# Expert tiles of a fused attention and mixture kernel: how many buffers each pool has, in which slots the loads are emitted, and both halves of the second expert layer ahead of the first combine

## The chip, the cores and the metric

One core of one Trainium2 chip runs the whole program. The metric is the device time of one execution in microseconds. Before the change the median of three runs is 944.0 us (943.19 to 945.39).

## What is computed

Three layers follow one another. The sizes are 4 batches, 8 heads, 768 positions, 64 per head, so 3072 tokens of 512 features.

```python
# 1. attention with 4 sink positions and a window of 128
keep = is_sink | ((rel >= 0) & (rel < window))
a = softmax(where(keep, q @ k.T / sqrt(64), -1e9)); x = a @ v        # (3072, 512)
# 2. gated layer, d_ff 1536
x = (sigmoid(x @ w_gate) * (x @ w_val)) @ w_out
# 3. soft mixture: 8 experts of 4 slots
logits = x @ phi                                                     # (3072, 32)
slot_in = softmax(logits, axis=0).T @ x                              # (32, 512)
for e in range(8): slot_out[e] = relu(slot_in[e] @ w1[e]) @ w2[e]    # w1 512x1024, w2 1024x512
out = softmax(logits, axis=1) @ slot_out                             # (3072, 512)
```

## The kernel before, in words

**Halves and passes.** The tokens are worked in 8 halves of 384 (half of a batch). The gated layer goes in five passes over the 12 chunks of its hidden features (128 each): half 0, halves 1 and 2, 3 and 4, 5 and 6, half 7 (line 437). Each pass loads its 36 weight tiles of 256 KB anew. They are numbered by chunk over all passes: g50, v50 and o50 are the tiles of the gate, the value and the output weight of chunk 50, and the last pass has chunks 48 to 59. Every tile comes by a DMA on SP's queue into one of three buffers `raw` (line 462), ACT copies its high part and POOL makes the low part by subtraction (lines 494 and 495); the buffer is then free for the load three tiles on. The products with the gate and value tiles are L632, those with the output tiles L670.

**Slots.** A list `ops` written out by hand (lines 593 to 596) holds 354 operations, each of them one group of L632 or L670. The main loop (line 1033) goes through it, and in every slot it also emits, where they are due, attention pieces, pieces of the third layer's logits and sums for a finished half (`m2`, lines 688 to 756), a splitting of `x`, one start of a weight tile with the next load, and at most one load of an expert tile (lines 1070 to 1073). The last pass begins in slot 294; a step of one chunk there is five slots.

**Order on the queues.** What the loop writes is the program's order only. The context is opened with `schedule_with_timeline_sim=True` (line 1137), and the order in which the instructions stand on each engine is fixed when the program is built; only those marked `pin` keep the order in which they are written. On the chip every engine then works off its queue in that order.

**Expert tiles.** The weights of the experts are 32 tiles of 1 MB (8 KB in each partition), in the order of line 801: 16 of `w1` (rows of 2 KB), then 8 of the left half of `w2` and 8 of its right half (rows of 1 KB). `NX = [10, 5, 8]` gives the number of buffers of three pools. Pool `xe0` opens when the attention is done and its memory is given back (line 1063; slot 290), and lies where the attention's tiles were. Pool `xe1` opens when the pass before the last is done (line 1067; slot 306). It begins where `xe0` ends, and its five tiles reach over the memory of `gv2`, `gv3` and `o3`, weight pools of the earlier passes. Behind those lie `ye` (the layer's output of the even halves) and `x0` (the input of every other half). Pool `x2` opens in the tail, on the memory of the last pass, from `x0` upwards. The 15 tiles of the first two pools are loaded in the loop, the other 17 in the tail: 8 into `x2`, then 9 into buffers 1 to 9 of `xe0` again as the first expert layer is done with them (lines 1083 to 1087). Buffer 0 takes the activations (`big`).

**Tail.** The last half's `m2` (its last step adds to `acc`, L752), then the weights of the combination (L828 to L833), the first expert layer (L857), and for each of two column halves c: `second(c)` (L878, then a small product L885 and copies L883 to L889 that make `S4[c]`), `combine(c)` (L896: 12 pairs of products, one copy each by DVE or ACT in turns, L900, and a store of 768 KB after every third, L902). The eight output tiles `ob` use the buffers of `x2`, each its own.

```python
        for q in range(len(xe)):
            if 32 - len(e_order) in range(sum(NX[0:q]), sum(NX[0:q + 1])):
                e_load(e_tile(xe[q], f"e{q}", NX[q]))
                break
```

Of the kernel before, what the change touches and what calls it, by code (L numbers as in the profile page):

```python
# [36 lines left out]
def fused_kernel(ctx, tc, qT, kA, kB, vB, vS, wg, wv, wo, phi, w1, w2, n_sink, window, out):  # L37
# [10 lines left out]
    def ps(tag, bufs, dt=F32):  # L48
        return psum.tile([128, 512], dt, name=tag, tag=tag, bufs=bufs)
# [122 lines left out]
    def tick():  # L172
        run = []
        for e in pend:
            e[0] -= 1
            if e[0] <= 0:
                run.append(e)
        for e in run:
            pend.remove(e)
            e[1]()  # L180
# [7 lines left out]
    def copy(eng, o, i):  # L188
        if eng is act:
            act.copy(o, i)  # L190
        else:
            eng.tensor_copy(o, i)  # L192
# [364 lines left out]
    def x_can():  # L557
        k = xs_n[0]
        return k < NH and k - 2 < xused[0] and done_half[0] > x_order[k]
# [238 lines left out]
    e_order = deque()  # L798
# [16 lines left out]
    def e_tile(pl, tag, bufs):  # L815
        return pl.tile([128, 2048], F32, name="ew", tag=tag, bufs=bufs)
# [6 lines left out]
    def combine_weights(cp, cT):  # L823

        for h in range(NH):
            c4 = cp.tile([128, 3, 4, 32], F32R, name="c4", tag="c4", bufs=2)
            cb = c_all[:, h].unsqueeze(2).to_broadcast([128, 3, 2, 32])
            dve.tensor_copy(c4[:, :, 0::2, :], cb)  # L828
            dve.tensor_tensor(c4[:, :, 1::2, :], cb, c4[:, :, 0::2, :].bitcast(F32), op=ALU.subtract)
            t = ps(("xt", "pt")[h % 2], 1)  # L830
            for i in range(3):
                pe.transpose(t[:, 128 * i:128 * i + 128].bitcast(F32R), c4[:, i].rearrange("p a b -> p (a b)"), identr)
            act.copy(cT[:, h, :], t[:, 0:384])  # L833

    def tail(ta, cp, big, outs):

        cT = cp.tile([128, NH, 384], F32R, name="cT")
        combine_weights(cp, cT)
        A = ta.tile([128, 2, 4, 4, 32], F32, name="A")
        pool.memset(A, 0.0)  # L840
        si_ps = ps("gv", 3)
        for d in range(4):
            pe.matmul(si_ps[:, 32 * d:32 * d + 32], acc[:, 128 * d:128 * d + 128], Rf[:, 0, :], start=True, stop=True,
                      skip_group_check=True)
        for g in range(2):
            dve.tensor_tensor(
                A[:, g, :, :, 4 * g:4 * g + 4],
                si_ps[:, 0:128].rearrange("p (d g j s) -> p g j d s", d=4, g=2, j=4)[:, g],
                zi.rearrange("p (g j s) -> p g j s", g=2, j=4)[:, g].unsqueeze(2).to_broadcast([128, 4, 4, 4]), op=ALU.mult)

        hTs = big().rearrange("p (g f r) -> p g f r", g=2, f=8)
        for g in range(2):
            hp = [ps("ys", 3) for _ in range(2)]
            for nn in range(2):
                for d in range(4):
                    for j in range(4):
                        pe.matmul(hp[nn][32 * j:32 * j + 32, :], A[:, g, j, d, :], xp[0, g, 4 * nn + d][:, j, :],  # L857
                                  start=(d == 0), stop=(d == 3), skip_group_check=True)
            hT = hTs[:, g]
            for nn in range(2):  # L860
                hs = ta.tile([128, 512], F32, name="hs", tag="hs", bufs=2)
                if nn:
                    act.activation(out=hs, in_=hp[nn], func=ACTF.Relu)
                else:
                    dve.tensor_scalar(hs, hp[nn], 0.0, None, op0=ALU.max)
                t = ps("gv", 3)
                for f in range(4):
                    pe.transpose(t[:, 128 * f:128 * f + 128], hs[:, 128 * f:128 * f + 128], ident)
                copy((dve, act)[nn], hT[:, 4 * nn:4 * nn + 4, :], t.rearrange("p (a b) -> p a b", a=4))

        S4 = {}

        def second(c):
            so = ps(("xt", "pt")[c], 1)
            for f in range(8):
                for g in range(2):
                    for j in range(4):
                        pe.matmul(so[32 * j:32 * j + 32, 0:256], hTs[:, g, f, 32 * j:32 * j + 32], xp[1, c, f][:, 4 * g + j, :],  # L878
                                  start=(f == 0 and g == 0), stop=(f == 7 and g == 1), skip_group_check=True)

            hs = ta.tile([128, 512], F32, name="hs", tag="hs", bufs=2)
            sos, S4h = hs[:, 0:256], hs[64:128, 256:512].bitcast(F32R)
            dve.tensor_copy(sos, so[:, 0:256])  # L883
            s4 = ps("ys", 3)
            pe.matmul(s4[:, 0:256], R2.rearrange("p a b -> p (a b)"), sos, start=True, stop=True)  # L885
            S4[c] = ta.tile([128, 256], F32R, name="S4", tag="S4", bufs=2)
            act.copy(S4h, s4[64:128, 0:256])
            dve.tensor_copy(S4[c][0:64], s4[0:64, 0:256])
            dve.tensor_tensor(S4[c][64:128], s4[64:128, 0:256], S4h.bitcast(F32), op=ALU.subtract)  # L889

        def combine(c):
            for t in range(NBLK // 2):
                o = ps("gv" if t % 2 else "ys", 3)
                for r in range(2):
                    h, i = divmod(2 * t + r, 3)
                    pe.matmul(o[:, 256 * r:256 * r + 256], cT[:, h, 128 * i:128 * i + 128], S4[c], start=True, stop=True,  # L896
                              skip_group_check=True)
                if t % 3 == 0:
                    ob = outs(NBLK // 6 * c + t // 3)[:, 0:1536].rearrange("p (r c) -> p r c", r=6)
                copy(act if t % 2 else dve, ob[:, 2 * (t % 3):2 * (t % 3) + 2, :], o.rearrange("p (r c) -> p r c", r=2))  # L900
                if t % 3 == 2:
                    sp.dma_start(out=out[256 * t - 512:256 * t + 256, 256 * c:256 * c + 256].rearrange("(r p) c -> p r c", p=128), in_=ob)  # L902

        for c in range(2):
            second(c)
            combine(c)


# [118 lines left out]

    setup_merge()
    credit = 0.0
    NX = [10, 5, 8]  # L1030
    xe = []
    e_reset()
    for k, (si, o, i) in enumerate(ops):
        phase[0] = steps[si][0][0] // NF
        if o == "y":
            if si:
                gemm2(si - 1, i)
        else:
            gemm1(si, i, o)
        tick()  # L1040
        now[0] = k + 1
        rate = 0.0
        for h in range(NH):
            todo = half_at[h] - emitted[0] - credit
            if todo > 0 and due[h] > now[0]:
                rate = max(rate, todo / max(due[h] - (3 if h == 1 else 5) - now[0], 1))
        credit += rate
        while credit >= 1:
            credit -= 1
            attn_piece()  # L1050
        if m2:
            m2_piece()
            if si == NS - 1:
                m2_piece()
        if x_can():
            x_split()
        if at_tasks:
            run_split()
        w_slot()
        if not xe and len(tops) == 1 and ws_n[0] >= 3 * NF and not w_fly:  # L1060
            top.close()
            tops.append(top.enter_context(tc.tile_pool(name="parts", bufs=1)))
        if not xe and not pieces and xs_n[0] == NH:
            top.close()
            left.close()
            xe.append(ctx2.enter_context(tc.tile_pool(name="xe0", bufs=1, reuse_waits="tile")))
        if len(xe) == 1 and min(gdone[0], ydone[0]) >= N_LEAN - 1 and m2_done[0] == NH - 1:
            inner.close()
            xe.append(ctx2.enter_context(tc.tile_pool(name="xe1", bufs=1, reuse_waits="tile")))
        for q in range(len(xe)):  # L1070
            if 32 - len(e_order) in range(sum(NX[0:q]), sum(NX[0:q + 1])):
                e_load(e_tile(xe[q], f"e{q}", NX[q]))
                break
    for i in range(3):
# [6 lines left out]
    ta = ctx2.enter_context(tc.tile_pool(name="ta", bufs=1, side="right", reuse_waits="tile"))  # L1081
    x2 = ctx2.enter_context(tc.tile_pool(name="x2", bufs=1, side="right", reuse_waits="tile"))
    for i in range(NX[2]):
        e_load(e_tile(x2, f"e2{i}", 1))
    big = e_tile(xe[0], "e0", NX[0])
    e_all(xe[0], "e0", NX[0], NX[0] - 1)
    e_all(xe[1], "e1", NX[1], 32)
    tail(ta, x2, lambda: big, lambda n: e_tile(x2, f"e2{n}", 1))
    ctx2.close()
    with tc.If(fast == 0):  # L1090
        general()
# [50 lines left out]
```

## Time and profile before

| | |
|---|---|
| median of 3 runs | 944.0 us |
| the profiled execution | 944.22 us |
| its span in the profile | 942.3 us |
| PE busy (products) | 898.0 us, 95% |
| DVE, POOL, ACT busy | 598.7, 475.9, 372.4 us |
| DMA | 133.40 MB, 142 GB/s in the mean |
| chain that ended last | PE 78%, DVE 8%, DMA 4%, issue 4%, ACT 3% |

PE is TensorE's products and PEld its weight loads; SPq is SP's queue, on which all DMAs of this kernel stand. The chain that ended last is followed back from the last instruction, at each step to what released it. The span lies 1.9 us below the time of the same execution. "Granted clock" (PEclk) is the share of full speed that TensorE had.

### The profile page before, as it was taken

How to read it: one execution, taken by the hardware profiler on the slowest of the kernel's cores; microseconds unless marked ns; L12 is line 12 of the kernel's file. 1: busy time of each engine (PE TensorE's matmuls, PEld its weight loads, DVE VectorE, ACT ScalarE, POOL GpSimd, SP SyncE). 2: the span in 40 equal slices, each digit the busy share in tenths (PEclk: the TensorE clock that was granted, in tenths of full speed). 3: DMA queues.
4: the chain of work that ended last, by engine and by line, in shares of the span. 5: the costliest groups of instructions: out<-in, count | busy, mean ns of one | idle time of the engine just before them, and what ended most of it. 6: DMA issues, size and time to landing. Idle time of an engine off the chain costs nothing.

```text
span 942.3 us, 15253 instructions
## 1 busy us (share of the span) xinstructions
PE 898.0 (95%) x5276; PEld 712.5 (76%) x5277; DVE 598.7 (64%) x1536; ACT 372.4 (40%) x996; POOL 475.9 (51%) x428
## 2 busy tenths in 40 slices
PE   8789998989999999999999999999999999899894
PEld 4455554556789999888889999898999987798452
DVE  8996869666558757765776767766455533444532
ACT  5675565333343343344343443343332323241221
POOL 3753445463346675655675756654644422684000
PEclk7799999999999999999999999999999999999897
DMA  6884657531213232333232333231212169656997
GB/s 230 285 268 154 226 173 230 165 100 44 68 54 103 82 106 54 106 84 99 59 105 68 98 78 96 77 101 55 79 57 68 45 211 387 230 155 196 310 323 236
DMA packets 80355, 133.40 MB, mean 142 GB/s; under 512 B 6800, under 2 KB 38544, under 8 KB 80272
## 3 DMA queue, kind: packets, MB, share of 16 engines
q1 hardware_dynamic: 80272, 132.37, 46.1%
q8 instruction: 43, 0.70, 0.3%
q14 instruction: 40, 0.33, 0.1%
HBM read 116.62 MB, written 15.73 MB: 140 GB/s over the span
## 4 chain that ended last, share of the span: by engine, by line
PE 78%; DVE 8%; DMA 4%; issue 4%; ACT 3%; POOL 1%; SPq 0%; POOLq 0%; DVEq 0%; ACTq 0%
PE gv L632 39%; PE ys L670 20%; PE ys L300 4%; PE xt L392 4%; DMA wraw<-wsv 2%; PE ys L857 2%; PE pt L367 2%; DVE wA L517 2%; DVE wA L518 1%; PE ys L697 1%; PE xt L395 1%; PE ys L706 1%; DVE wA L521 1%; PE xt L878 1%; DMA wbits<-in_wv_dram 1%
## 5 line engine op out<-in xcount | busy, mean ns | idle before, releaser
L632 PE MATMUL gv<-xh,whv 128*128 128x384 f32 x432 | 151.6, 379 | 3.2 <-ACT whv L190 3.2
L632 PE MATMUL gv<-xh,whg 128*128 128x384 f32 x432 | 153.1, 383 | 0.0
L670 PE MATMUL ys<-who,gh 128*128 128x512 f32 x324 | 140.2, 460 | 7.8 <-DVE ysb L675 6.3
L649 POOL TENSOR_TENSOR gl<-th,gh 128x384 fp32r<-128x384 f32 x84 | 89.3, 1063 | 111.8 <-DVE gh L192 95.0
L675 DVE SCALAR_TENSOR_TENSOR ysb<-ys,ysb 128x512 f32<-128x512 f32 x138 | 93.0, 683 | 37.8 <-PE ys L670 37.1
L632 PE MATMUL gv<-xh,wlv 128*128 128x384 f32 x336 | 114.3, 340 | 0.7 <-POOL wlv L495 0.7
L632 PE MATMUL gv<-xl,whv 128*128 128x384 f32 x336 | 114.3, 340 | 0.0
L632 PE MATMUL gv<-xl,whg 128*128 128x384 f32 x336 | 114.0, 339 | 0.0
L632 PE MATMUL gv<-xh,wlg 128*128 128x384 f32 x336 | 113.3, 337 | 0.0
L321 ACT ACTIVATE PC<-P,nb 128x132 f32<-128x132 f32 (+1 forms) x152 | 60.2, 397 | 109.0 <-DVE P L315 77.7
L670 PE MATMUL ys<-wlo,gh 128*128 128x512 f32 x252 | 99.5, 395 | 0.0
L670 PE MATMUL ys<-who,gl 128*128 128x512 f32 x252 | 98.4, 396 | 0.0
L632 PEld LDWEIGHTS gv<-xh,whv 128*128 128x128 f32 x432 | 81.3, 190 | 20.0 <-issue 6.4
L327 POOL TENSOR_TENSOR PC<-PC,sm 128x264 f32<-128x264 f32 (+1 forms) x76 | 50.3, 663 | 90.4 <-DVE sm L326 68.3
L632 PEld LDWEIGHTS gv<-xh,whg 128*128 128x128 f32 x432 | 81.7, 191 | 16.0 <-issue 4.7
L495 POOL TENSOR_TENSOR wlv<-wraw,whv 128x512 fp32r<-128x512 f32 x48 | 63.0, 1313 | 58.6 <-ACT whv L190 54.0
L670 PEld LDWEIGHTS ys<-who,gh 128*128 128x128 f32 x324 | 60.2, 189 | 36.6 <-issue 18.2
L645 DVE SCALAR_TENSOR_TENSOR th<-th,gv 128x384 f32<-128x384 f32 x84 | 46.3, 551 | 61.4 <-PE gv L632 50.5
L495 POOL TENSOR_TENSOR wlg<-wraw,whg 128x512 fp32r<-128x512 f32 x48 | 62.5, 1302 | 34.1 <-ACT whg L190 26.9
L304 DVE CUSTOM_DVE_ANT_0 P<-ys,mask 128x260 f32<-128x260 f32 (+1 forms) x152 | 57.2, 392 | 34.1 <-PE ys L300 34.0
L636 ACT ACTIVATE th<-gv 128x384 f32<-128x384 f32 x96 | 46.8, 487 | 80.4 <-PE gv L632 79.8
L325 DVE TENSOR_SCALAR sm<-sm 128x2 f32<-128x2 f32 x96 | 35.9, 374 | 63.5 <-ACT PC L321 57.9
(211 smaller groups left out, 1834.7 us busy)
## 6 DMA issues: line engine op xcount, KB each, us to landing
ew<-in_w_dram SPq DMA_DIRECT2D x32, 1024.0 KB, 12.1
wraw<-wsg SPq DMA_DIRECT2D x48, 256.0 KB, 2.7
wraw<-wsv SPq DMA_DIRECT2D x48, 256.0 KB, 2.7
wraw<-wso SPq DMA_DIRECT2D x48, 256.0 KB, 2.7
wbits<-in_wg_dram SPq DMA_DIRECT2D x12, 512.0 KB, 4.2
wbits<-in_wv_dram SPq DMA_DIRECT2D x12, 512.0 KB, 4.6
wbits<-in_wo_dram SPq DMA_DIRECT2D x12, 512.0 KB, 4.7
out_dram<-ew SPq DMA_DIRECT2D x8, 768.0 KB, 6.8
```

Of the source, the lines that this page charges most:

```text
L300: pe.matmul(Ss[h][:, 0:w], QK[n][0][h][:, 128 * jj:128 * jj + 128], k[h][:, w0:w0 + w], start=(i == 0), stop=(i == len(QK[n]) - 2))
L304: dve.tensor_tensor_reduce(out=P[:, h, 0:w], in0=S[:, 0:w], in1=mask[:, MOFF[mt]:MOFF[mt] + w], scale=-0.125, scalar=3.0e38, op0=ALU.add, ...
L321: act.activation(out=dst[:, h], in_=src[:, h], func=ACTF.Exp, scale=-1.0, bias=nb[:, h:h + 1], accum_out=sm[:, h:h + 1])
L327: pool.tensor_tensor(dst, dst, sm.unsqueeze(2).to_broadcast([128, 2, src.shape[2]]), op=ALU.mult)
L392: pe.matmul(xt[64 * h:64 * h + 64, cols], VT[n][:, jj + s - i, 64 * h:64 * h + 64], pts[:, i, h, :], start=(jj == 0 and i == 0), stop=Fals ...
L495: pool.tensor_tensor(lo, r, hi.bitcast(F32), op=ALU.subtract)
L632: pe.matmul(acc_ps[:, 0:384], wt[:, 128 * d:128 * d + 128], xt[:, d, :], start=(k == 0), stop=(k == 4 * len(seq) - 1))
L636: act.activation(out=th, in_=acc_ps[:, 0:384], func=ACTF.Tanh, scale=0.5)
L645: dve.scalar_tensor_tensor(gr, th, 1.0, acc_ps[:, 0:384], op0=ALU.add, op1=ALU.mult)
L649: pool.tensor_tensor(gl, gr, gh.bitcast(F32), op=ALU.subtract)
L670: pe.matmul(yp, a[:, 128 * i:128 * i + 128], w, start=(k == 0), stop=(k == len(seq) * len(ns) - 1))
L675: dve.scalar_tensor_tensor(ysb[h][:, i, :], yp, 0.5, ysb[h][:, i, :], op0=ALU.mult, op1=ALU.add)
```

## The change

The three pools get 12, 5 and 6 buffers in place of 10, 5 and 8. An expert tile is emitted in the loop only in slots whose number is a multiple of 3. The output tiles 6 and 7 take the buffers of output tiles 0 and 1. `second(1)` is emitted ahead of `combine(0)`. By the slots, the loads now stand at 291, 294, ... 324 for `xe0` and 327 to 339 for `xe1`, where they stood at 290 to 299 and 306 to 310; with 12 tiles of 8 KB in `xe0`, `xe1` lies 16 KB higher and now reaches over `gv2`, `gv3`, `o3`, `ye` and `x0`. All 17 are emitted ahead of the tail, which has 15 left: 6 into `x2`, 9 into `xe0`.

```diff
         for c in range(2):
             second(c)
+        for c in range(2):
             combine(c)
...
-    NX = [10, 5, 8]
+    NX = [12, 5, 6]
...
         for q in range(len(xe)):
-            if 32 - len(e_order) in range(sum(NX[0:q]), sum(NX[0:q + 1])):
+
+            if k % 3 == 0 and 32 - len(e_order) in range(sum(NX[0:q]), sum(NX[0:q + 1])):
                 e_load(e_tile(xe[q], f"e{q}", NX[q]))
                 break
...
-    tail(ta, x2, lambda: big, lambda n: e_tile(x2, f"e2{n}", 1))
+    tail(ta, x2, lambda: big, lambda n: e_tile(x2, f"e2{n % NX[2]}", 1))
```

## Rows read from the trace of the kernel before

**Rows 1.** The page: TensorE's granted clock and DMA rate, 40 equal slices

```profile
PEclk7799999999999999999999999999999999999897
...
GB/s 230 285 268 154 226 173 230 165 100 44 68 54 103 82 106 54 106 84 99 59 105 68 98 78 96 77 101 55 79 57 68 45 211 387 230 155 196 310 323 236
```

**Rows 2.** Stretches: busy PE, PEld, DVE, ACT, POOL; clock, DMA share, GB/s

```profile
790.00:795.00 5.00, 5.00 (x34) 4.34 (x33) 1.38 (x2) 2.01 (x4) 0.00 (x0) 1.00 1.05 387
...
810.00:815.00 5.00, 1.80 (x7) 1.48 (x8) 0.71 (x2) 1.85 (x3) 2.51 (x3) 0.92 0.21 75
815.00:820.00 5.00, 5.00 (x23) 5.00 (x22) 1.44 (x2) 1.53 (x3) 3.98 (x5) 0.74 0.61 167
...
855.00:860.00 5.00, 5.00 (x29) 4.86 (x28) 1.98 (x4) 1.12 (x2) 2.66 (x3) 1.00 1.02 330
...
880.00:885.00 5.00, 4.80 (x26) 3.12 (x30) 3.37 (x15) 0.86 (x2) 0.00 (x0) 0.50 1.09 348
```

**Rows 3.** SP's queue from 749 to 812 us: start, us, line, DMA, count

```profile
763.35 20.02 SPq L812 DMA_DIRECT2D ew<-in_w_dram  x10
783.47 2.52 SPq L463 DMA_DIRECT2D wraw<-wsv  x1
...
787.77 11.19 SPq L812 DMA_DIRECT2D ew<-in_w_dram  x5
801.47 0.49 SPq L463 DMA_DIRECT2D wraw<-wsv  x1
```

**Rows 4.** The chain that ended last, 783 to 822 us: start, us, what

```profile
783.47 12.39 DMA wraw<-wsv
...
801.47 10.30 DMA wraw<-wsv
```

**Rows 5.** PE in order of time, 796 to 815 us; in brackets idle before

```profile
799.61 1.06 PE L750 MATMUL ys<-ysb,ET 128*32 128x512 f32 x6 [0.38 <-ACT ET L730]
...
802.45 0.34 PE L632 MATMUL gv<-xh,wlv 128*128 128x384 f32 x1
...
812.47 0.44 PE L632 MATMUL gv<-xh,whv 128*128 128x384 f32 x1 [3.21 <-ACT whv L190]
...
813.82 0.45 PE L632 MATMUL gv<-xh,wlv 128*128 128x384 f32 x1 [0.74 <-POOL wlv L495]
```

**Rows 6.** DVE in order of time at the start of the span

```profile
1.46 0.17 DVE L132 MEMSET ones<- 96x128 f32 x1
```

**Rows 7.** DMA issues about 852 us: count, KB each, us to landing

```profile
ew<-in_w_dram SPq DMA_DIRECT2D x1, 1024.0 KB, 6.4
```

**Rows 8.** SP's queue in the tail

```profile
852.13 54.77 SPq L812 DMA_DIRECT2D ew<-in_w_dram  x17
915.38 16.48 SPq L902 DMA_DIRECT2D out_dram<-ew  x8
```

**Rows 9.** The chain that ended last, from 904 us

```profile
904.28 6.66 PE xt L878 x120
...
914.47 0.24 PE gv L896 x2
...
917.80 5.36 PE pt L878 x96
...
923.67 0.71 PE ys L885 x2
...
925.86 0.47 PE ys L896 x2
...
930.50 0.59 ACT ew L190
```

**Rows 10.** The page, DMA issues: count, KB each, median us to landing

```profile
out_dram<-ew SPq DMA_DIRECT2D x8, 768.0 KB, 6.8
```

**Rows 11.** The chain that ended last, one step of the last pass to the next

```profile
853.44 1.63 PE ys L670 x7
...
859.72 1.63 PE ys L670 x7
```

## The prediction

> **What bounds the kernel now.** I read the page's slices first. TensorE is at full clock and almost always busy, so time can only be lost where PE waits; and the DMA rate, near 80 GB/s for most of the span, has two hills: one at slices 33 to 35 (up to about 811 us), the first block of expert tiles, and one in the tail [rows 1]. So I cut these stretches fine. From 790 to 795 us the DMAs run flat out at 387 GB/s; right behind that hill, from 810 to 815, PE is busy 1.80 of 5 us, and from 815 to 820 its clock is 0.74; later, from 855 to 860, PE is busy all the time though the DMAs are full again [rows 2]. So the first hill costs PE time and the start of the tail's hill does not.
>
> SP's queue tells why. Ten expert tiles stand in one block at 763.35, and the load of v50 behind them at 783.47; then five more, and v51 behind those at 801.47 [rows 3]. Weights and experts share one queue: v50 lands 12.39 us after its issue, at 795.87, and v51 10.30 us after, at 811.77 [rows 4]. PE gets v50 just in time (the product at 802.45 follows without idle time) and v51 too late: 3.21 us of idle time, then 0.74 until its low part is made [rows 5].
>
> One more row decides what follows. The constants of L132 are emitted only when the first half's attention is written, yet they are set at 1.46 us [rows 6]. So the place in a queue is not the place in the program: what has its buffer and its data free goes ahead of anything that still waits. The ten tiles show the same. By the slots v50's load (slot 297) belongs behind the seventh, but it waited for a raw buffer, and all ten went first [rows 3].
>
> **The change part by part.**
>
> *One load in three slots.* The tiles of `xe0` wait for the attention's memory only; when that is free, all of them are. I expect the spacing to vanish on the queue as the order of slots 290 to 299 did, and cost it at nothing, gain or loss. The cover is the empty stretch of SP's queue while v50 waits for its raw buffer; if the order is kept instead, that is the first rival.
>
> *Twelve tiles in the first block.* A tile is 1.05 MB, at 387 GB/s 2.71 us [rows 2]. Two more put v50's landing 5.4 us later, at 801.3. From v51's landing to the first product with its low part went 2.05 us (811.77 to 813.82) [rows 4, 5]; so v50 is ready at 803.3 where PE took it at 802.45 [rows 5]: +0.9 us, contained in the next term.
>
> *Five tiles behind it, 16 KB higher.* `xe1` now covers `ye`, whose last reader is the sum of half 6 on PE, 799.61 to 800.67 [rows 5]. Since the pool was handed out as one before (all five in a row, rows 3), I let all five wait for that. The queue has run empty by then: 801.3 and two weight tiles of 0.26 MB, 0.68 us each, give 802.7. A tile issued on an almost empty queue took 6.4 us to land [rows 7]; so the first of the five lands at about 807.1, four more take 10.8, v51 behind them 0.68: 818.6 in place of 811.77, **+6.8 us**. Without the new wait, counting bytes alone, it would be 802.7 + 5 × 2.71 + 0.68 = 816.9, +5.1. I take 6.8, since the wait is on the memory that the pool covers. Queued behind the five on SP are v51, o51 and g52; PE waits for v51. Later PE has no gap that could give this back (855 to 860, as an instance) [rows 2]. The trace shows 387 GB/s [rows 2].
>
> The Trainium skill (DMA: Bandwidth & Descriptors, Specifications) puts a core's share of HBM at about 358 GB/s. By that a tile would take 2.93 us, seven of them 1.5 us more, and the whole sum 951.8; the measured rate decides.
>
> *The clock.* After the idle time of before, 1.7 us were lost to the lower level, 1.2 GHz in part of these stretches (5 × 0.08 and 5 × 0.26, rows 2). The idle time grows from 4 to about 10 us. It costs nothing more at the least; at the most what the tail's long sparse stretch lost, 2.5 us in 880 to 885 [rows 2] and about 1 around it, so 1.7 more. I take +0.5, near the lower end, because the half clock starts with the idle time and part of it falls in it.
>
> *Two tiles fewer in the tail.* The first tail loads are issued from 852.13 on [rows 8], where PE is busy 5.00 of 5 us [rows 2]: leaving two out gives 0. The later ones wait for the last pass's memory and follow one another as now. So the right half of `w2` arrives no sooner against PE.
>
> *`second(1)` ahead of `combine(0)`.* On PE 24 products, on DVE and ACT 12 copies, on SP four stores move behind second(1)'s 128 products and its four copies; all loads stand ahead of them on SP already (issued by 906.90, rows 8), POOL has no part in it. Between the end of second(0) at 910.94 and the last 96 products of second(1) at 917.80 PE has 6.86 us; 32 products of second(1) at 0.056 (5.36 us / 96), L885 with 0.71 and 24 products of combine at 0.12 fill 5.4 [rows 9]. So 1.4 us can be gained at the most on PE. If combine(0) goes behind altogether, its copies run at combine(1)'s pace, 4.6 us (925.86 to 930.50) [rows 9], second(1) ends at 918.9, and both combines at 928.1, 2.4 us earlier; but the first store goes out at about 920.5 in place of 915.38 [rows 8], and eight of 0.79 MB at 387 GB/s take 16 us and more, to about 939 to 942 against a span of 942.3. I take −1.0, and −2.5 to +2.0 for the range. The new wait of output tile 6 for store 0 (6.8 us after its issue [rows 10], so about 927) is met when its copy is due at about 927; if not, DVE's and ACT's remaining copies queue behind it, up to 2 us, within that range.
>
> **The sum.** 944.2 + 6.8 + 0.5 − 1.0 = 950.5 in the profiled execution's own time; this execution is 0.2 us above the median of 944.0, so 950.3 us.
>
> **Rivals.**
>
> *The spacing holds* (faster). Tiles and weights alternate, v50 and v51 come in time. Back comes the idle time of 3.95 and the clock's 1.7, and 1.0 in the tail: 937.4. But a step of 6.3 us [rows 11] would then carry 0.79 MB of weights and 1.75 MB of tiles, 403 GB/s against 387, a lag of 0.26 us per step over some seven steps: about 939. For it: the code says so. Against it: rows 3 and 6. It decides where v50's load stands behind two or three tiles on SP. By this rival the hill at 763 would be a plateau to about 860.
>
> *The five of `xe1` part into two groups* (near even). Some of its buffers do not touch `ye`; with v51 between them the two short delays could hide behind the three raw buffers: about +1, 945. Against it: before, all five stood in a row though some lay on other memory [rows 3].
>
> *A costlier stall* (slower still). A gap of 10 us also empties POOL and ACT, and v52 and v53 come late too: up to 4 us more, 955. For it: right behind the gap POOL is busy 3.98 of 5 us [rows 2], with little room to catch up.
>
> **How the numbers follow.** Forecast 0.70, spacing 0.15, two groups 0.10, costlier 0.05. The forecast's own range is 946.6 (5.1, 0, −2.5) to 954.5 (6.8, 1.7, +2.0). To hold 8 in 10 I go down to the two groups and up to the costlier stall: 943 to 956; outside is the spacing. About 0.2%, 1.9 us, is what a measurement here can tell from no change. Faster: spacing, and a little of the two groups, 0.16. Same: most of the two groups, 0.07. Slower: forecast, costlier, the rest, 0.77.
>
> **What would show it.** Right: SP's queue has twelve tiles in one block, v50's load behind them at about 788.7; v51 lands near 818; PE's idle time ahead of v51's products is near 9 us; the tail's loads start with 15; `second(1)` ends about 1 us sooner after `second(0)`. Wrong: fewer than ten tiles ahead of v50, no idle time at L632 between 800 and 820, or the hill of rows 1 flattened to some 300 GB/s over four slices.

## The result, and the profile after

The changed kernel takes 958.34 us (957.55 to 961.09, 4 runs) against 944.69 us (943.19 to 947.58, 4 runs): ratio 1.0147, 95% interval 1.0119 to 1.0174. Timed once more beside other kernels it took 955.99 us against 944.07, ratio 1.0122 (1.0105 to 1.0138). So the change costs about 12 to 14 us. The prediction had it slower, at 950.3 us and at most 956.0, so the direction came and the size did not; the second timing lies at the very end of that range.

The profiled execution took 961.09 us, its span is 959.2. Its page, the slices that answer to [rows 1]:

```profile
PEclk8689999979999999999999999999999999799896
...
GB/s 230 298 261 131 231 161 244 153 99 34 67 56 103 89 105 67 103 77 76 63 110 78 113 53 109 84 90 41 59 78 67 45 345 386 180 145 145 333 190 266
```

Two things stand out. The first hill of the DMA rate is longer (345 and 386 where before had 211 and 387). And the end has a new hole: 190 in the slice before the last. SP's queue, the rows that answer to [rows 3] and [rows 8]:

```profile
763.12 0.32 SPq L463 DMA_DIRECT2D wraw<-wsg  x1
767.38 25.69 SPq L812 DMA_DIRECT2D ew<-in_w_dram  x12
793.17 1.08 SPq L463 DMA_DIRECT2D wraw<-wsv  x1
...
797.73 10.91 SPq L812 DMA_DIRECT2D ew<-in_w_dram  x5
808.74 3.70 SPq L463 DMA_DIRECT2D wraw<-wsv  x1
...
869.91 47.85 SPq L812 DMA_DIRECT2D ew<-in_w_dram  x15
935.52 13.85 SPq L902 DMA_DIRECT2D out_dram<-ew  x8
```

Twelve tiles stand in one block, v50's load behind them, then five and v51's: the spacing by slots is not there. The eight stores are one block that starts at 935.52, where before the first left at 915.38.

The spans differ by 16.9 us, more than the timed runs do, so I cut both at two events that every kernel here has: the issue of the first expert load, and DVE's first copy L883, the end of `second(0)`. Before, they are at 763.35 [rows 3] and at

```profile
910.96 0.43 DVE L883 COPY hs<-xt 128x256 f32<-128x256 f32 x1 [7.11 <-PE xt L878]
```

In the table A runs from the start of the span to the first event, B from there to the second, C to the end. The kernels below `after` are the experiments.

| kernel | A | B | C | B against before | C against before |
|---|---|---|---|---|---|
| before | 763.4 | 147.6 | 31.3 | | |
| after | 767.4 | 154.0 | 37.9 | +6.4 | +6.5 |
| change_again | 764.9 | 154.0 | 37.9 | +6.4 | +6.6 |
| loads_only | 767.2 | 154.0 | 30.1 | +6.4 | -1.3 |
| order_only | 762.3 | 147.5 | 38.0 | -0.1 | +6.6 |
| third_only | 767.2 | 147.3 | 31.1 | -0.3 | -0.2 |
| order_s4 | 761.4 | 147.7 | 31.1 | +0.1 | -0.2 |
| change_s4 | 763.3 | 154.0 | 30.1 | +6.4 | -1.2 |

A is not the change's doing: SP's queue is the same up to the first expert load, and `third_only`, which has before's instructions in before's order on SP, DVE, ACT and POOL, has an A of 767.2 too. Of the 4.0 us of `after`, 2.6 arise on SP's queue between 207 and 232 us, behind a stretch in which TensorE had less of its full clock and PE was less busy (columns as in [rows 2]). Before:

```profile
195.00:205.00 10.00, 8.75 (x31) 4.46 (x31) 6.04 (x19) 4.19 (x12) 6.69 (x7) 0.83 0.34 87
```

After:

```profile
195.00:205.00 10.00, 7.29 (x14) 4.09 (x15) 6.45 (x17) 2.53 (x8) 6.66 (x7) 0.59 0.41 109
```

So the change has two costs of nearly the same size: 6.4 us in B, which the loads make, and 6.5 us in C.

**B.** The rows of PE that answer to [rows 5], in order of time, with the idle time in brackets:

```profile
803.64 1.06 PE L750 MATMUL ys<-ysb,ET 128*32 128x512 f32 x6 [0.38 <-ACT ET L730]
...
822.18 0.69 PE L632 MATMUL gv<-xh,whv 128*128 128x384 f32 x1 [7.76 <-ACT whv L190]
823.54 0.69 PE L632 MATMUL gv<-xh,wlv 128*128 128x384 f32 x1 [0.34 <-POOL wlv L495]
```

PE waits 7.76 us for v51's high part where it waited 3.21; the product with the low part runs at 823.54, in before's time (less 4.03, by which A is longer) 819.51, 5.7 us later than at 813.82. The DMAs show no gap ahead of that; the 365 GB/s in the second row are those of the last of the five tiles, the first of `w2`, with its rows of 1 KB (stretches in the columns of [rows 2]):

```profile
809.00:814.00 5.00, 4.86 (x25) 4.21 (x24) 0.92 (x3) 0.49 (x1) 2.26 (x3) 1.00 1.05 388
814.00:819.00 5.00, 0.43 (x2) 0.00 (x0) 1.89 (x3) 0.00 (x0) 0.00 (x0) 0.90 1.07 365
819.00:824.00 5.00, 1.47 (x3) 0.96 (x4) 0.00 (x0) 1.80 (x3) 1.79 (x2) 0.50 0.33 119
824.00:829.00 5.00, 5.00 (x19) 5.00 (x19) 1.11 (x2) 1.45 (x3) 4.10 (x4) 0.58 0.53 159
```

The clock falls to its lower level while PE stands still, and it is not back when PE is busy again: half of the 0.46 us from 823.54 to 824 and 0.42 of the 5 us behind it are 2.3 us. Before, behind the product at 813.82, 0.08 and 0.26 of 5 us were lost, 1.7 us [rows 2]. These 0.6 and the 5.7 of the late tile make 6.3 of the 6.4.

**C.** The tail in the same columns. First the two stretches of before that correspond to the first two of after:

```profile
915.00:920.00 5.00, 5.00 (x74) 3.32 (x76) 2.90 (x5) 2.40 (x5) 0.00 (x0) 1.00 0.77 247
920.00:925.00 5.00, 3.82 (x62) 1.90 (x54) 0.57 (x2) 0.37 (x1) 0.00 (x0) 1.00 1.04 347
```

After:

```profile
925.00:930.00 5.00, 4.80 (x60) 2.77 (x55) 0.00 (x0) 3.13 (x6) 0.00 (x0) 1.00 0.03 12
930.00:935.00 5.00, 3.64 (x45) 2.21 (x34) 2.10 (x5) 0.37 (x1) 0.00 (x0) 1.00 0.00 0
...
945.00:950.00 5.00, 0.00 (x0) 0.00 (x0) 0.00 (x0) 0.00 (x0) 0.00 (x0) 0.50 1.04 343
```

The DMAs are empty for some 10 us, then nothing but the stores is left, at 343 GB/s, with all engines idle. DVE in order of time shows what the stores waited for. Before, three copies of `combine(0)` follow `S4[0]` at once, and three more well ahead of `second(1)`'s sums at 923.19:

```profile
914.03 1.89 DVE L192 COPY ew<-ys 128x512 f32<-128x512 f32 x3 [0.59 <-PE ys L896]
916.65 2.00 DVE L192 COPY ew<-ys 128x512 f32<-128x512 f32 x3 [0.73 <-PE ys L896]
```

After:

```profile
924.50 0.43 DVE L889 TENSOR_TENSOR S<-ys,hs 64x256 fp32r<-64x256 f32 x1
931.83 0.42 DVE L883 COPY hs<-pt 128x256 f32<-128x256 f32 x1 [6.90 <-PE pt L878]
933.28 0.69 DVE L192 COPY ew<-ys 128x512 f32<-128x512 f32 x1 [1.02 <-PE ys L896]
933.88 0.41 DVE L888 CAST S<-ys 64x256 fp32r<-64x256 f32 x1
934.30 0.43 DVE L889 TENSOR_TENSOR S<-ys,hs 64x256 fp32r<-64x256 f32 x1
934.76 6.07 DVE L192 COPY ew<-ys 128x512 f32<-128x512 f32 x10
```

`S4[0]` is ready at 924.93, but DVE makes no copy of `combine(0)` until `second(1)` is done: the first at 933.28, the others behind `S4[1]`. PE says why: of `combine(0)` it runs only the products into `gv`; every `ys` product stands behind L885 of `second(1)`.

```profile
925.43 0.98 PE L896 MATMUL gv<-S,cT 128*128 128x256 f32 x6
...
932.30 0.70 PE L885 MATMUL ys<-hs,R 128*128 128x256 f32 x2 [0.55 <-DVE hs L883]
932.65 0.82 PE L896 MATMUL ys<-S,cT 128*128 128x256 f32 x4
```

### The profile page after: what moved, and what is told of

Read it like the earlier page. It is cut to its first block, busy times and chain, and to the rows that moved or that the text cites. A ratio compares the mean times of both kernels' runs of the same rounds, so it can differ in the third digit from the quotient of the medians.

```text
span 959.2 us, 15252 instructions
## 1 busy us (share of the span) xinstructions
PE 906.1 (94%) x5277; PEld 715.7 (75%) x5277; DVE 594.9 (62%) x1536; ACT 373.1 (39%) x996; POOL 475.6 (50%) x428
## 4 chain that ended last, share of the span: by engine, by line
PE 80%; DVE 7%; DMA 6%; issue 3%; ACT 2%; POOL 1%; SPq 0%; ACTq 0%; POOLq 0%; DVEq 0%
PE gv L632 40%; PE ys L670 20%; PE ys L300 5%; PE xt L392 4%; PE ys L857 2%; PE pt L367 2%; DMA wraw<-wsv 1%; DMA wraw<-wso 1%; DVE wA L517 1%; PE ys L697 1%; PE xt L395 1%; PE ys L706 1%; DVE wA L518 1%; PE pt L878 1%; PE xt L878 1%
## 5 line engine op out<-in xcount | busy, mean ns | idle before, releaser
L632 PE MATMUL gv<-xh,whv 128*128 128x384 f32 x432 | 153.6, 384 | 7.8 <-ACT whv L190 7.8
L325 DVE TENSOR_SCALAR sm<-sm 128x2 f32<-128x2 f32 x96 | 33.2, 346 | 61.5 <-ACT PC L321 56.0
## 6 DMA issues: line engine op xcount, KB each, us to landing
ew<-in_w_dram SPq DMA_DIRECT2D x32, 1024.0 KB, 12.9
```

The source lines that it names most:

```text
L632: pe.matmul(acc_ps[:, 0:384], wt[:, 128 * d:128 * d + 128], xt[:, d, :], start=(k == 0), stop=(k == 4 * len(seq) - 1))
```

## The experiments

### The two halves of the change apart

`order_only` is the kernel before with this edit alone:

```diff
             second(c)
+        for c in range(2):
             combine(c)
```

> The kernel before with one edit: both halves of the second layer ahead of the first combine; tiles and slots stay. Theory: of the 16.9 us between the two profiled spans, 6.6 arise behind the last loads, because no store goes out while second(1) runs: in the changed kernel the DMAs moved 12 GB/s from 925 to 930 us and nothing from 930 to 935, and the first store was issued at 935.52, 9.8 us later than before counted from the loads of the tail. So this kernel takes about 951 us (944.7 + 6.6), with eight stores in a row and the DMAs empty for some 10 us ahead of them. It has eight tiles in the tail, so no output tile waits for a store; if the wait for stores 0 and 1 made the loss, the time is near 944. If the late weights made it all, it is near 944 too. The prediction on record gave this step -1.0: 943.7.

Measured: 952.08 us against 944.59, ratio 1.0073 (1.0050 to 1.0095), 6.9 us by the ratio. C is 6.6 us longer, B is not. Its tail has eight output tiles, so no copy waits for a store: the wait for stores 0 and 1 is not the cause. SP:

```profile
924.21 13.87 SPq L902 DMA_DIRECT2D out_dram<-ew  x8
```

ACT, which copies the `gv` products, is through with all six of `combine(0)` by 916.3, so half of that combine's copies are made 8 us before the first store (the last three of them):

```profile
914.70 1.56 ACT L190 COPY ew<-gv 128x512 f32<-128x512 f32 x3 [0.35 <-PE gv L896]
```

`loads_only` is the changed kernel with the old order of `second` and `combine`:

```diff
             second(c)
-        for c in range(2):
             combine(c)
```

> The changed kernel with the old order of second and combine: twelve, five and six tiles, one slot in three, output tiles 6 and 7 in the places of 0 and 1. Theory: what is left is the late landing of v51, 5.7 us by the start of the load behind it on SP's queue (9.7 late, of which 4.0 stood there since 257 us), and about 0.6 of half clock: 944.7 + 6.3 = 951.0. If the loss of the tail came from the loads' side (six tiles, two output tiles that wait for stores), the time stays near 958. The prediction on record gave these steps +7.3: 952.

Measured: 949.73 us, ratio 1.0042 (1.0020 to 1.0063). B is 6.4 us longer, as expected, and PE waits once for v51 (what PE waited for: us in total, times, longest):

```profile
PE gv L632 <- ACT whv L190: 7.8, 1, 7.8
```

C is 1.3 us shorter than before, which was not expected. B and C together cost 5.1 us, and the timed cost is 4.0 by the ratio. Of the 1.3, 1.0 lies in `second(1)`: DVE copies its sums at 932.33, 11.2 us behind those of `second(0)` at 921.14, where before took 12.2 (923.19 and 910.96). Why it ends sooner is open.

`third_only` is the kernel before with the condition on the slot:

```diff
-            if 32 - len(e_order) in range(sum(NX[0:q]), sum(NX[0:q + 1])):
+            if k % 3 == 0 and 32 - len(e_order) in range(sum(NX[0:q]), sum(NX[0:q + 1])):
```

> The kernel before with the condition on the slot alone (one load in three slots, ten and five tiles). Theory: the place in the program does not set the place in SP's queue, since all tiles of the pool wait for the same memory; ten tiles in one block, then v50's load, then five; 944.7 us and the same rows. It is also a measure of how far two executions of one order of work differ. If spacing had an effect of its own, fewer than ten tiles would stand ahead of v50's load and the idle time of 4 us in 805 to 815 would shrink: 939.

Measured: 943.72 us, ratio 0.9973 (0.9951 to 0.9996). In its profile SP, DVE, ACT and POOL have the instructions of before in the same order (one load of a flag at the very end apart), and the block is there:

```profile
767.16 19.90 SPq L812 DMA_DIRECT2D ew<-in_w_dram  x10
```

So one load in three slots does nothing by itself. The interval leaves out 1 though the two programs do the same: a difference of 0.3% between two kernels is not to be read here, even behind an interval.

### Why the stores came late

`order_s4` adds one edit to `order_only`:

```diff
-            s4 = ps("ys", 3)
+            s4 = so[:, 256:512]
```

> The first kernel of this set (order alone) with one more edit: the small product of R2 goes into the free half of second's own PSUM bank instead of one of the three ys buffers. Theory: the ys buffers are handed out in the order of the program, so the combine's ys tiles come after the one that second(1) takes for this product, and stand behind second(1) on PE and DVE; with that one gone, the six ys copies of combine(0) run before second(1) ends and the first store goes out near 915 to 918: 942 to 945 us. If instead the order of the program itself puts combine(0) behind second(1) (or DVE's copy of second(1)'s sums, which would still stand there), the time is that of the order alone, about 951.

Measured: 945.08 us, ratio 0.9996 (0.9973 to 1.0019): the whole loss of the order is gone. DVE:

```profile
911.11 0.43 DVE L889 TENSOR_TENSOR S<-xt,hs 64x256 fp32r<-64x256 f32 x1
912.13 1.89 DVE L192 COPY ew<-ys 128x512 f32<-128x512 f32 x3 [0.59 <-PE ys L896]
914.76 2.00 DVE L192 COPY ew<-ys 128x512 f32<-128x512 f32 x3 [0.74 <-PE ys L896]
921.29 0.42 DVE L883 COPY hs<-pt 128x256 f32<-128x256 f32 x1 [4.54 <-PE pt L878]
```

```profile
913.48 16.14 SPq L902 DMA_DIRECT2D out_dram<-ew  x8
```

All six copies stand ahead of `second(1)`'s again, though the program still names `second(1)` first. That fits this explanation: the three `ys` buffers go to their takers in the program's order. With `second(1)` named first, its product L885 takes one ahead of the `ys` tiles of `combine(0)`, and these can have their place on the queues only behind it. Without that taker they are hoisted to where their data are ready. Why even those `ys` tiles stand behind L885 for which the other two buffers would have done, no run shows apart. The rival, that the order of the program itself keeps `combine(0)` back, falls. The edit takes nothing away from the work, so the cause is L885's place among the takers of `ys`. The order then gains nothing either: C is 0.2 us shorter than before.

`change_s4` makes the same edit in the changed kernel.

> The changed kernel whole, with the product of R2 in the free half of second's own PSUM bank. Theory: the loss of the tail goes, as it did with the order alone, and that of the weights stays: 944.7 + 4 to 6 = 949 to 951, first store right behind second(0), no more than 2 us apart from the kernel with the loads alone. Here output tiles 6 and 7 lie where 0 and 1 did; if their wait for the stores matters once the stores go out early, the time is up to 2 us more.

Measured: 950.98 us, ratio 1.0078 (1.0048 to 1.0107), with the B and C of `loads_only` within 0.1 us. By the ratio that is 7.4 us (4.5 to 10.1) where `loads_only` gave 4.0 (1.9 to 6.0); the two profiles agree, and put what the loads cost at some 5.2 us. C stays below before's, though output tiles 6 and 7 lie in the places of 0 and 1.

### Whether loads that are really apart would pay

In `apart_3` and `apart_4` (ten and five tiles) and in `apart_3_more` (twelve, five and six) each load waits for its slot. The tile gets one element of the newest `gh` first, which the load overwrites:

```diff
+            last[0] = gh
...
-            if 32 - len(e_order) in range(sum(NX[0:q]), sum(NX[0:q + 1])):
-                e_load(e_tile(xe[q], f"e{q}", NX[q]))
+            if k % 4 == 0 and 32 - len(e_order) in range(sum(NX[0:q]), sum(NX[0:q + 1])):
+                t = e_tile(xe[q], f"e{q}", NX[q])
+                act.copy(t[0:1, 0:1], last[0][0:1, 0:1].bitcast(F32))
+                e_load(t)
                 break
```

`k % 3` in the other two; `apart_3_more` also has the change's `NX` and output tiles.

> The kernel before (ten and five tiles, old order of second and combine) with a load in one of four slots, and with each load made to wait for its slot: ACT copies one element of the newest gh into the tile first, so the load can't leave before that gh is made. Theory: weights and tiles now alternate on SP's queue, one or two tiles between weight loads (0.79 MB of weights and 1.3 MB of tiles in a step of 6.3 us, 333 GB/s, below the 387 that the DMAs moved), so v51's weights come in time: the 4 us of idle time ahead of the products and 1.7 us of half clock go, 939 us. Rival: the block of ten only fills time in which nothing else could have been loaded, and what waits behind it comes no sooner, since a tile's load that waits for its slot also holds up the weights behind it on the same queue: 944 or more, with new idle time of PE at weight products between 765 and 850.

> As the one before, with a load in one of three slots, as the change has it. Theory: 0.79 MB of weights and 1.75 MB of tiles in a step of 6.3 us are 403 GB/s against 387, so a lag of some 0.3 us a step builds up over six or seven steps, less than the lead of the raw buffers: 939 to 941. Rival as above: 944 or more.

> Twelve, five and six tiles, one slot in three, each load made to wait for its slot by the same small copy, old order of second and combine. Theory: the loss of these tile numbers comes only from the two blocks on the queue; taken apart, they cost nothing: 939 to 942. If they lose by something else (the memory that the five lie on, the tail with six tiles), the kernel stays 4 to 5 us above the one with ten and five tiles under the same condition.

Measured: `apart_4` 947.79 us, ratio 1.0034 (1.0011 to 1.0057); `apart_3` 943.21, ratio 0.9990 (0.9965 to 1.0015); `apart_3_more` 950.11, ratio 1.0072 (1.0048 to 1.0096). The queue is as it was meant to be, a few rows of `apart_3`:

```profile
787.12 0.34 SPq L463 DMA_DIRECT2D wraw<-wsv  x1
787.56 0.38 SPq L814 DMA_DIRECT2D ew<-in_w_dram  x1
797.41 0.32 SPq L463 DMA_DIRECT2D wraw<-wsv  x1
797.83 0.94 SPq L814 DMA_DIRECT2D ew<-in_w_dram  x2
```

and PE's one long wait is gone, but short ones have come at other weights (us in total, times, longest):

```profile
PE gv L633 <- ACT whg L190: 4.2, 4, 1.4
```

The theory of 939 us falls, the rival stands, if only just in `apart_3`, for which it gave 944 or more: idle time of one kind was traded for idle time of another. In these runs the first tile itself waits, so A and B do not compare; from the load of g50 (759.09 before) to the end of `second(0)` it is 151.9 us before, 151.6 in `apart_3`, 155.6 in `apart_4` and 158.1 in `apart_3_more`. A raw buffer is free again only when its tile has landed and been split, so a tile of 2.71 us [rows 2] ahead of a weight holds back not only this weight but also the load three behind it; that link was argued from the queue and not tried apart. In `apart_3_more` I was wrong altogether: 17 tiles cost some 7 us more than 15 even without the blocks, and 6.2 of them lie in that stretch, as much as the blocks cost. Here it is the end of the pass, where two tiles were issued at 850.91 among the last weights, PE stood idle for 3.9 us and the clock fell:

```profile
860.00:865.00 5.00, 1.10 (x4) 0.50 (x3) 1.55 (x3) 1.83 (x3) 1.33 (x2) 0.79 0.45 168
865.00:870.00 5.00, 5.00 (x16) 5.00 (x17) 1.20 (x2) 1.24 (x2) 3.72 (x4) 0.52 0.29 105
```

`five_apart_4` and `five_apart_6` leave the ten in one block and take only the five of the second pool apart (`if q:` ahead of the small copy; the condition on the slot, modulo 4 or 6, for the second pool only).

> The kernel before with only the five tiles of the second pool taken apart: they wait for slots that are four apart, by the copy of one element of gh ahead of each load; the ten stay one block. Theory: v50 comes as before, v51 stands behind no tile but one and comes in time, so 4.0 us of idle time and 1.7 us of half clock go, and the five share the DMAs with weights where these are half idle (144 to 167 GB/s from 815 to 850 us): 939 to 941 us. Rival, as in the runs with all tiles apart: a tile that waits for its slot on SP holds up the weight loads behind it, and the idle time comes back in pieces of 1 to 1.5 us at other weight products: 943 to 946.

> As the one before with slots six apart, so that between two tiles stand three or more weight loads and the DMAs have time to spare. Theory: 939 to 941, as above. Rival: 943 to 946; and if the pieces of idle time come from the share of the DMAs rather than from the queue, this one is faster than the one with four.

Measured: 946.28 us, ratio 1.0011 (0.9995 to 1.0027), and 947.79, ratio 1.0017 (0.9994 to 1.0039). The wait at v51 went in both, and nothing was won: B is 147.6 us in the first, that of before, and 149.5 in the second. Nor is the one with slots six apart the faster, as it would be if the share of the DMAs made the idle time. That time lies elsewhere; in `five_apart_4` its largest piece is at 825 to 830, where the DMAs at 143 GB/s are far from full:

```profile
825.00:830.00 5.00, 2.87 (x15) 2.23 (x14) 0.28 (x1) 2.28 (x6) 2.61 (x3) 1.00 0.38 143
```

`eight_five` is the kernel before with `NX = [8, 5, 8]`.

> The kernel before with eight and five tiles ahead of the tail (the tail loads 19). The second pool then lies 16 KB lower, on memory that is free when the first pool's is, so I expect all thirteen in one block ahead of v50, and none between v50 and v51. Theory (a weight is late by the bytes that stand ahead of it, 2.71 us for a tile): v50 lands 8.1 us later than before and PE, which took it just in time, stalls some 6 to 8 us there, v51 then comes without a second stall, so 4.0 and 1.7 us go; from the queue alone +1 to +2. Two more tiles in the tail: 0 if the loads of the tail that wait for the last pass's memory set its end, up to 6 us if the bytes do. 945 to 952. If a block ahead of a weight costs PE nothing until v51, the time is 939 to 945.

Measured: 946.30 us, ratio 1.0014 (0.9991 to 1.0038). The thirteen stand in one block as expected:

```profile
767.69 26.79 SPq L812 DMA_DIRECT2D ew<-in_w_dram  x13
...
809.27 0.44 PE L632 MATMUL gv<-xh,whv 128*128 128x384 f32 x1 [1.97 <-ACT whv L190]
810.62 0.44 PE L632 MATMUL gv<-xh,wlv 128*128 128x384 f32 x1 [0.73 <-POOL wlv L495]
```

The stall at v50 is 2.7 us, not the 6 to 8 that I gave: I had left out most of the lead that PE has there: v50's 795.87 and the 2.05 us to its low part make 797.9, its product ran at 802.45, and 8.1 less 4.5 is 3.6. No version here beats the kernel before by more than a measurement can tell.

### The change once more

> The changed kernel once more, with the same number of rounds as its parts. Theory: its parts add up, the late weights 4 to 5 us (loads_only) and the stores behind second(1) 6.9 (order_only), so 944.6 + 11 to 12 = 956 to 957 us; if it stays at 958.3 or more, the two losses lengthen each other by some 2 us, as in the profiled execution, where the tail of the kernel with the loads alone got 1.5 us back that the changed one did not.

Measured: 955.99 us, ratio 1.0122 (1.0105 to 1.0138), 11.5 us by the ratio, where the two parts give 4.0 + 6.9 = 10.9. They add up within their intervals. In the profiles the order costs 7.8 us of C on top of the loads (37.9 against 30.1) and 6.6 alone, so they lengthen each other by about 1 us.

## Why the prediction was wrong

**The spacing has no effect: right.** Twelve tiles in one block, v50's load at 793.17, less 4.03 that is 789.1 (788.7 was given), and `third_only` shows it alone. The first rival falls twice: the spacing does not hold, and where it is forced it does not bring the 5 us that I gave it.

**Twelve tiles in the first block: right.** v50 with its low part was ready for PE at 803.8 in before's time (803.3 was given), and PE waited 0.45 us for it. The term that counts is the next one.

**The five wait for L750, +6.8: the reason was wrong, the size near.** Only a part of the five waited (SP's queue by what it waited for: us in total, times, longest):

```profile
SPq L812 <- PE ys L750: 3.7, 1, 3.7
```

Two had been issued ahead of it, and the queue did not run empty as I had assumed: the DMAs moved 385 GB/s and more from 794 to 814 us. My own numbers said as much: the wait ends at 800.67, and the bytes ahead last until 802.7. So the bytes alone count, my lower bound of 5.1, against 5.7 measured at the product with v51's low part. The rival of two groups is borne out in the parting of the five, but v51's load stands behind all of them, not between. By the Trainium skill (DMA: Bandwidth & Descriptors, Specifications) a core's share is about 358 GB/s, half of what one stack gives two cores. One core alone runs here, and the trace shows more for these loads (388 in 809 to 814); the measurement decides.

**The clock, +0.5, and two tiles fewer in the tail, 0: near.** The clock cost 0.6 by the rows above; with v51 it makes 7.3 forecast for B against 6.4 measured. The reason that I gave for the clock does not hold: before, the lower level did not start with the idle time. The 0.92 of 810 to 815 [rows 2] is 0.8 us of it, so it began at 814.2, when PE was busy again; after, by the 0.90 of 814 to 819, at 818.0, some 4 us into the idle time. The tail of the kernels with the loads came out 1.2 to 1.3 us shorter, as long as the order was the old one or had its buffer; with the new order, 37.9 against 38.0, that gain is gone.

**`second(1)` ahead of `combine(0)`, -1.0 with bounds -2.5 and +2.0: this step failed**, by 7.5 us: C grew by 6.5. In the profiles B and C miss by 6.6 together (12.9 against 6.3), since B came 0.9 below its forecast; the first timing misses by 8.0, and the 1.4 more lie in neither. What PE was to gain is there: `second(1)` ends at 931.76, 10.4 us after `second(0)` (DVE's copy at 921.35), against 12.2 before (923.16 and 910.96), 1.8 us sooner. And I had named nearly the case that came, combine(0) altogether behind second(1); only its `gv` half still stood ahead. But I mis-sized it.

First, "the first store goes out at about 920.5": it went out at 935.52, which is 925.1 when counted from the end of `second(0)`, 4.6 us later than I gave. With the `gv` products still ahead, `second(1)` ended at 921.4 in that count and not at 918.9; and the store left 3.8 us behind that end and not 1.6, since the `ys` copies had to wait for L885 and most of them for `S4[1]` as well. Second, I held "about 939 to 942" for the last landing against the end of the span, 942.3, but before's last store had landed at 939.97, so even my own case meant -1 to +2, and I took -1.0. The stores needed 21.5 us from the first issue to the last landing. My "16 us and more" used 387 GB/s, a rate of loads with rows of 2 KB, but 939 to 942 left room for 21.5. 925.1 and 21.5 make 946.6, 6.6 us behind 939.97.

I had counted products and copies and looked at no PSUM buffer: the row that could have warned me was L885's own, whose output is `ys` [rows 9], the same three buffers that L896 takes turns on.

**The new wait of output tiles 6 and 7.** I had expected it to be met in time. It was not, but it costs nothing that can be seen: C is 37.9, and 38.0 in `order_only`, which has no such wait. One copy on DVE:

```profile
941.78 0.69 DVE L192 COPY ew<-ys 128x512 f32<-128x512 f32 x1 [0.95 <-DMA out_dram<-ew]
```

Two copies on ACT wait in the same way. The stores ahead keep the DMAs busy to the end anyway. The rival of a costlier stall is not borne out either: 955 came out near the measured time, but the loss it named, v52 and v53 late, is not in the profile, whose B is 6.4.

## What to carry to other kernels

When a piece of work is moved ahead of another, list the buffers that each takes from a shared ring, PSUM's too: a small product that takes its turn early can hold back everything behind it, on engines that the move does not touch. The Trainium skill (Perfetto Trace Analysis, Matmuls) wants independent groups of products to rotate through PSUM banks so that the copies of one run beside the products of the next. The trace agrees: in `order_s4` the six `ys` copies of `combine(0)`, 912.13 to 916.76, run while PE goes on with products. It also shows the other side, that one taker in the rotation with late data stops the ones behind it (8.4 us without a `ys` copy, from 924.93 to 933.28, and none of it when that taker left the ring).

Where the last transfers set the end, ask first when the first of them leaves and what rate they run at, by rows of such transfers and not of others. And a queue that is fixed when the program is built does not follow the slots in which its loads are written: only a dependency moves a load, and what it then holds back on its own queue counts as well.

## What was not expected of the hardware

One order of work differs by several us from one execution to the next, and in these profiles always early: the time up to the first expert load was 761.4 to 769.1 us in profiles of kernels that do the same up to there, while the stretches behind it repeated within 0.4 us in kernels with the same loads. Cutting the span at an event that both kernels have removed this; comparing whole spans would have put 4 us to the change that are not its own.

Large transfers do not all run at one rate here. Tiles with rows of 2 KB came in at 385 to 388 GB/s (387 in 790 to 795 before [rows 2]; 385 to 388 from 794 to 814 after). The tail's tiles of `w2`, with rows of 1 KB, came in at 348 (880 to 885 [rows 2]), and the stores of 768 KB, with rows of 1 KB too, went out at 331 to 347 with nothing beside them. So the difference goes more with the rows than with the direction; no run changes one of the two alone.
